# Expert weights kept in DRAM once as float32 and split into two parts when a unit is loaded

## The chip, the cores and the metric

The kernel runs on one core of one Trainium2 chip. The time is the device time of one execution in microseconds. The engines are called PE (TensorE), DVE (VectorE), ACT (ScalarE), POOL (GpSimd) and SP (SyncE, which here only issues DMAs).

## What is computed

Eight batches of attention whose 12 heads are mixed before and after the softmax, and behind it an expert layer on the 3584 tokens.

```python
scores = scale * np.matmul(q, k.transpose(0, 1, 3, 2))         # 8 x 12 x 448 x 448
scores = np.einsum('bhij,hg->bgij', scores, w_pre)
attn = softmax(scores)
attn = np.einsum('bhij,hg->bgij', attn, w_post)
x = np.matmul(attn, v)                                          # -> 3584 x 768
a, b = x @ w1, x @ w2                                           # 768 -> 1024
out = ((a * b) @ w3) @ w_out                                    # 1024 -> 1024 -> 768
```

## The kernel before

**Attention** goes in steps n; tile m of two blocks of 10 rows takes the two steps 2m and 2m+1. An even step fetches raw scores (`fetch`, L201), takes the largest value (`largest`, L226, DVE) and the exponentials (`exp`, L234, ACT); an odd step scales (`scale`, DVE and POOL), then multiplies with the second mixing matrix (`post`, L259, PE) and the next tile with the first (`mix`, L219, PE), copies the results (`put`, L273, ACT), and makes raw scores of the next batch (`qk`, L173, with two ACT copies, L178 and L179). `av` (L300) multiplies with v.

**The expert layer** is written as a generator whose steps are single PE matmuls. Each step n of the attention takes a number of them (`advance`), half before the exponentials are written and half behind, so expert matmuls fill PE between the attention's. The order in which instructions are written is the order on each engine; there is no planner. After the last attention step the rest runs alone, six matmuls at a time (the tail).

Matmuls take float32 numbers in two parts: `hi`, the number rounded by a copy to the type fp32r, and `lo`, the rest, by a subtract. Each product is three matmuls, hi x hi, hi x lo and lo x hi.

**Weights.** w3 and w_out are folded into one matrix at the start (`folding`, L359); w1 and w2 come as int64 words that are converted on the chip (`converting`, `to_f32`). Batches 0 and 1 go through the experts one at a time (`expert_atoms`, L521 and L552); batches 2 to 7 in three pairs (`pair_experts`), by a scheme with seven products m = 1 to 7 per block of two by two in place of eight (`layer`, L701). It needs sums of weight blocks; these are made once, while batch 1 passes (`seen`, `sums`).

A *unit* is the piece of weights of one matmul group or of half of one, 128 x 384 or 128 x 512 numbers in two parts. `wp` holds unit tiles (`wu`). `next_unit` hands out the next one and asks for a further load, which SP issues in the next step (`do_later`). At most `w_ahead` (3; for the pairs 4, in the tail 7) units are loaded or asked for ahead. A group's result stands in one of the two PSUM banks 6 and 7 in turn; `gather` (L655, DVE; its first product L657, ACT) adds it to an accumulator and frees the bank. It is written up to three matmuls after the next group has begun.

In DRAM everything lies in both parts: `w_d` (w1, w2), `w34_d` (the folded matrix), `s_d` (the sums). The parts are made where the numbers are made: by `two_parts` (ACT and POOL) for converted units, by an ACT copy and a DVE subtract for the folded matrix, by `split` (L482, L483: ACT and POOL) for the sums, eleven sets of four.

Of the kernel before, what the change touches and what calls it, by code (L numbers as in the profile page):

```python
# [49 lines left out]
class Kernel:  # L50
# [58 lines left out]
    def to_f32(self, s, m, name):  # L109
# [9 lines left out]
        x = self.cx.tile([128, CW], F32, tag="x", name=f"cx{name}")[:, :n]  # L119
# [227 lines left out]
    def folding(self):  # L347
        nc = self.nc
        for f in range(KF):
            for half in range(2):  # L350
# [10 lines left out]
                z = self.fp.tile([128, 3, 2, 128], F32R, tag="z", name=f"fz{half}_{f}")  # L361
                q = p.rearrange("p (d c) -> p d c", c=128)
                dst = self.w34_d[half * 3:(half + 1) * 3, :, f].rearrange("d p t c -> p d (t c)")

                def low(z=z, q=q, dst=dst):
                    nc.vector.tensor_tensor(z[:, :, 1], q, z[:, :, 0].bitcast(F32), op=ALU.subtract)
                    self.later.append(lambda: nc.sync.dma_start(dst, z.rearrange("p d t c -> p d (t c)").bitcast(F32)))

                self.ends.append((i, lambda z=z, q=q: nc.scalar.copy(z[:, :, 0], q)))
                self.soon.append((i, low))  # L370
# [17 lines left out]
    def load_unit(self):  # L388
        i = self.n_loaded
        t = self.wp.tile([128, KF // 2 * 256], F32R, tag="w", name=f"wu{i}")  # L390
        t, view, src = (self.unit_of_one if i < self.n_one else self.unit_of_pair)(t, *self.unit_list[i])
        self.nc.sync.dma_start(t.bitcast(F32), src)
        self.loaded.append(view)
        self.n_loaded += 1
        self.n_asked -= 1

    def unit_of_one(self, t, w, f, q):
        h = (K1 if w < 2 else KF) // 2
        t = t[:, :h * 256].rearrange("p (k t c) -> p k t c", k=h, t=2)
        return t, t, (self.w_d[w] if w < 2 else self.w34_d)[f][:, q * h:(q + 1) * h]  # L400

    def unit_of_pair(self, t, w, f, m):
        h, c = (K1 // 2, KF // 2) if w < 2 else (KF // 2, K1 // 2)
        t, src = t[:, :h * 256], self.w_d[w] if w < 2 else self.w34_d
        if m in (1, 2, 4):
            t = t.rearrange("p (k t c) -> p k t c", k=h, t=2)
            return t, t, src[f + c * (m == 4)][:, h * (m > 1):h * (1 + (m > 1))]
        return t, t.rearrange("p (t k c) -> p k t c", k=h, t=2), self.s_d[w][m][f]
# [8 lines left out]
    def unit_part(self, x, w, f, q):  # L417
        h = K1 // 2
        t = self.wp.tile([128, KF // 2 * 256], F32R, tag="w", name=f"wu{self.n_loaded}")
        t = t[:, :h * 256].rearrange("p (k t c) -> p k t c", k=h, t=2)  # L420
        self.loaded.append(t)
        self.n_loaded += 1
        self.two_parts(x, t[:, :, 0], t[:, :, 1])
        self.later.append(lambda: self.nc.sync.dma_start(self.w_d[w][f][:, q * h:(q + 1) * h], t.bitcast(F32)))

    def ask_units(self):
        while self.w_made <= self.n_loaded + self.n_asked < len(self.unit_list) and \
                len(self.loaded) + self.n_asked < self.w_ahead:
# [3 lines left out]
    def next_unit(self):  # L432

        t = self.loaded.pop(0)
# [33 lines left out]
    def sums(self, w, f, k):  # L468
# [8 lines left out]
        def split(m, i):  # L477
            s = self.cs.tile([128, CW, 2], I32, tag="s", name=f"s{w}_{f}_{m}", bufs=3)
            s = s.rearrange("p n b -> p (n b)").bitcast(F32)
            dst, x = self.s_d[w][m][f].rearrange("p (t n) -> p t n", t=2), y[:, i]  # L480
            hi, lo = s[:, :n], s[:, n:2 * n] if w < 2 else x
            nc.scalar.copy(hi.bitcast(F32R), x)  # L482
            nc.gpsimd.tensor_tensor(lo.bitcast(F32R), x, hi, op=ALU.subtract)  # L483
            if w < 2:
                self.later.append(lambda: nc.sync.dma_start(self.s_d[w][m][f], s))
            else:
                self.later.append(lambda: nc.sync.dma_start(dst[:, 0], hi))
                self.later.append(lambda: nc.sync.dma_start(dst[:, 1], lo))

        def first():  # L490
            sum(y[:, 0:2], y[:, 0:2], y[:, 2:4], ALU.subtract)

        def second():
            sum(y[:, 1:3], y[:, 1:3], y[:, 0::3], ALU.add)

        def third():
            sum(y[:, 3], y[:, 3], y[:, 0], ALU.subtract)


        splits = ((2, 7, 0), (3, 5, 2), (4, 3, 1), (5, 6, 3)) if w < 2 else ((3, 5, 2), (3, 3, 1), (4, 6, 3), (5, 7, 0))  # L500
        for delay, x in ((1, first), (2, second), (3 if w < 2 else 2, third)):
            self.at(delay, x)
        for delay, m, i in splits:
            self.at(delay, lambda m=m, i=i: split(m, i))
# [235 lines left out]
    def run(self):  # L740
# [9 lines left out]
        self.w_d = [dp.tile([KF, 128, k, 2, 128], F32, name=f"w{i}_d") for i, k in enumerate((K1, K1, KF))]  # L750
        self.x_d = [dp.tile([2, 128, K1 // 2, S], F32, name=f"x{b}_d") for b in range(B)]
        self.s_d = [{m: dp.tile([c, 128, k * 256], F32, name=f"s{i}_{m}_d") for m in (3, 5, 6, 7)}
                    for i, (c, k) in enumerate(((KF // 2, K1 // 2), (KF // 2, K1 // 2), (K1 // 2, KF // 2)))]
        self.w34_d = dp.tile([K1, 128, KF, 2, 128], F32, name="w34_d")
# [127 lines left out]
        self.loaded, self.n_loaded, self.n_asked, self.w_ahead = [], 0, 0, 3  # L882
# [5 lines left out]
        for n in range(N + 6):  # L888
# [4 lines left out]
            if n == SWITCH:  # L893
# [7 lines left out]
                self.wp = self.pool("wp", 5, side="right")  # L901
# [7 lines left out]
            if n == PAIR:  # L909
# [5 lines left out]
                self.pairs, self.w_ahead = True, 4  # L915
# [72 lines left out]
        self.wp, self.w_ahead = self.pool("wt", 8), 7  # L988
# [62 lines left out]
```

## Time and profile before

| | |
|---|---|
| three runs | 1453.31, 1459.1, 1459.4 us; median 1459.1 |
| profiled execution | 1456.61 us, span 1454.8 us, granted PE clock 0.985 |
| busy: PE, DVE, ACT, POOL | 1390.1, 739.0, 833.1, 620.7 us |
| DMA | 416.86 MB, mean 287 GB/s; HBM read 279.77 MB, written 134.09 MB |
| weight units loaded | 200 of 384 KB, 87 of 512 KB |

The span runs from the first to the last instruction of the profiled execution; the execution's time has 1.8 us more around it. Busy time is a union over the engine's instructions. In a list of waits each row names the engine and line that stood idle, what ended its wait, the sum in us, how often, and the longest. In a row of groups the number before the comma is busy time and the one after it the mean duration in ns. PE's busy time counts modelled ends of pipelined matmuls: one expert matmul stands with about 370 ns, but they start one every 0.2 us.

### The profile page before, as it was taken

The numbers are of one execution on the slowest core, as the hardware profiler recorded it, in microseconds if no ns is written. First come the engines' busy times: TensorE is split into PE (matmuls) and PEld (weight loads), VectorE is DVE, ScalarE is ACT, GpSimd is POOL, SyncE is SP. The second block draws the span as 40 slices with busy tenths as digits, with TensorE's granted clock in tenths as the row PEclk, the third lists the DMA queues.
The fourth block names the chain that finished last, engine by engine and source line by source line (L and its number), as shares of the span: only waits on it lengthen the run. The fifth ranks groups of instructions, "written<-read, shape, count | busy, mean of one in ns | idle before, by whom it ended". The sixth has DMA issues, their size and how long they took to land.

```text
span 1454.8 us, 45722 instructions
## 1 busy us (share of the span) xinstructions
PE 1390.1 (96%) x18684; PEld 1059.4 (73%) x18684; DVE 739.0 (51%) x1497; ACT 833.1 (57%) x1952; POOL 620.7 (43%) x754
## 2 busy tenths in 40 slices
PE   5789998999999989999999999999999999999998
PEld 2357785776677667776777777777776777899988
DVE  4867565767644544432344445334444447334563
ACT  3876665777756656665555656656655546422231
POOL 1333232444324434632244445444335446446683
PEclk7989998999999999999999999999999999999999
DMA  8998789999999999999989988799879766698875
GB/s 256 365 319 274 237 267 287 311 336 307 316 288 353 348 343 319 368 338 314 311 266 291 319 278 280 234 312 350 288 230 285 236 179 214 206 332 263 240 229 173
DMA packets 203760, 416.86 MB, mean 287 GB/s; under 512 B 20528, under 2 KB 120112, under 8 KB 203472
## 3 DMA queue, kind: packets, MB, share of 16 engines
q1 hardware_dynamic: 203552, 413.94, 87.2%
q8 instruction: 149, 2.44, 0.7%
q14 instruction: 59, 0.48, 0.1%
HBM read 279.77 MB, written 134.09 MB: 284 GB/s over the span
## 4 chain that ended last, share of the span: by engine, by line
PE 78%; DMA 13%; DVE 5%; ACT 3%; issue 1%; SPq 0%; POOL 0%; DVEq 0%; ACTq 0%; POOLq 0%
PE e L701 20%; PE psa L300 10%; PE pso L259 10%; PE psm L219 8%; PE psq L173 7%; PE psf L359 5%; PE eg L521 4%; PE e2o L701 4%; PE e1o L701 4%; PE e3o L701 4%; DMA s_d<-s 3%; PE eo L552 3%; DMA cs<-wo 3%; DMA r<-raw_d 2%; DMA wu<-w_d 2%; ACT e L234 1%
## 5 line engine op out<-in xcount | busy, mean ns | idle before, releaser
L246 POOL TENSOR_SCALAR w<-wpo,ri 128x60 f32<-128x60 f32 x360 | 180.7, 518 | 489.0 <-DVE ri L244 465.8
L226 DVE TENSOR_REDUCE mn<-psm 128x1 f32<-128x448 f32 x360 | 207.8, 619 | 317.0 <-PE psm L219 316.6
L701 PE MATMUL e<-eh,wu 128*128 128x448 f32 x1008 | 297.3, 372 | 6.3 <-DVE c L655 3.2
L273 ACT COPY mt<-pso 128x480 f32<-128x480 f32 x352 | 197.8, 621 | 177.3 <-PE pso L259 177.1
L234 ACT ACTIVATE e<-psm,mn 128x448 f32<-128x448 f32 x360 | 226.6, 642 | 9.6 <-DVE mn L226 9.6
L219 PE MATMUL psm<-r,wsc 60*64 60x448 f32 (+1 forms) x1440 | 197.9, 557 | 32.1 <-ACT e L234 19.9
L701 PEld LDWEIGHTS e<-eh,wu 128*128 128x128 f32 x1008 | 188.0, 188 | 52.5 <-issue 27.4
L259 PEld LDWEIGHTS pso<-w,e 60*64 60x64 f32 x10080 | 174.5, 134 | 50.0 <-issue 44.0
L259 PE MATMUL pso<-w,e 60*64 60x60 f32 x10080 | 198.6, 224 | 0.1
L701 PE MATMUL e<-el,wu 128*128 128x448 f32 x504 | 187.1, 371 | 0.0
L173 PE MATMUL psq<-kq 64*64 64x448 f32 x1176 | 159.5, 546 | 0.6 <-ACT st L178 0.6
L300 PE MATMUL psa<-mt,v 128*64 128x150 f32 (+1 forms) x2304 | 156.9, 293 | 1.9 <-ACT st L178 1.9
L300 PEld LDWEIGHTS psa<-mt,v 128*64 128x64 f32 x2304 | 143.6, 137 | 17.9 <-issue 6.3
L655 DVE TENSOR_TENSOR c<-c,e 128x448 f32<-128x448 f32 x168 | 101.8, 618 | 87.6 <-PE e L701 82.8
L178 ACT COPY st<-psq 128x448 f32<-128x448 f32 x162 | 86.4, 533 | 68.8 <-ACT mt L273 32.8
L521 PE MATMUL eg<-xh,wu 128*128 128x448 f32 x384 | 118.8, 380 | 4.8 <-DMA wu<-w_d 4.8
L640 POOL TENSOR_TENSOR el<-x,eh 128x448 fp32r<-128x448 f32 x90 | 104.2, 1176 | 34.8 <-ACT eh L639 34.8
L701 PEld LDWEIGHTS e<-el,wu 128*128 128x128 f32 x504 | 94.9, 188 | 22.4 <-issue 14.1
L243 DVE TENSOR_SCALAR sa<-sm 128x2 f32<-128x2 f32 x180 | 35.9, 200 | 129.6 <-ACT e L234 129.0
L173 PEld LDWEIGHTS psq<-kq 64*64 64x64 f32 x1176 | 62.2, 136 | 53.8 <-issue 29.8
L521 PEld LDWEIGHTS eg<-xh,wu 128*128 128x128 f32 x384 | 71.8, 190 | 38.1 <-issue 25.3
L179 ACT COPY st<-psq 128x448 f32<-128x448 f32 x162 | 87.7, 541 | 0.0
(99 smaller groups left out, 2011.5 us busy)
## 6 DMA issues: line engine op xcount, KB each, us to landing
r<-raw_d SPq DMA_DIRECT2D x344, 210.0 KB, 4.9
raw_d<-st SPq DMA_DIRECT2D x138, 448.0 KB, 5.4
wu<-w_d SPq DMA_DIRECT2D x104, 384.0 KB, 6.4
wu<-s_d SPq DMA_DIRECT2D x96, 384.0 KB, 4.8
wu<-w_d SPq DMA_DIRECT2D x51, 512.0 KB, 5.6
kq<-kq SPq DMA_DIRECT2D x42, 448.0 KB, 6.2
wu<-s_d SPq DMA_DIRECT2D x36, 512.0 KB, 4.9
x<-x_d SPq DMA_DIRECT2D x72, 224.0 KB, 6.3
```

Of the source, the lines that this page charges most:

```text
L173: nc.tensor.matmul(ps[s][z * PP:(z + 1) * PP], t[rows, q:q + PP], t[rows, k:k + S], start=True, stop=True)
L219: nc.tensor.matmul(ps[s][c * PP:(c + 1) * PP, :S], self.wsc[k], r[k, c], start=True, stop=True)
L226: self.nc.vector.tensor_reduce(mn[:, s:s + 1], self.psm[m][s][:, :S], axis=AX.X, op=ALU.min)
L234: nc.scalar.activation(e, p[:, :S], AF.Exp, bias=mn[:, s:s + 1], scale=-1.0, accum_out=sm[:, s:s + 1])
L246: nc.gpsimd.tensor_scalar_mul(w2[:, s], self.wpo, ri[:, s:s + 1])
L259: nc.tensor.matmul(self.pso[c][z * PP:(z + 1) * PP, at:at + HK], e[k, j * PP:(j + 1) * PP], w2s[k, s], start=True, stop=True)
L273: self.nc.scalar.copy(dst.rearrange("p j g (s i) -> p j s g i", s=2), src)
L300: nc.tensor.matmul(self.psa[rows, g % 3, :W], v[:, j, rows], mt[:, j, 2 * g + s, :W], start=(j == 0), stop=(j == NJ - 1))
L521: nc.tensor.matmul(p, u[:, k % (K1 // 2), x], xs[y][:, k], start=(k == 0 and t == 0), stop=(k == K1 - 1 and t == 2))
L640: nc.gpsimd.tensor_tensor(lo, x, hi.bitcast(F32), op=ALU.subtract)
L655: nc.vector.tensor_tensor(a[out], a[to[0]], p, op=ALU.add)
L701: nc.tensor.matmul(p, w[:, k, x], ops[m, k][y], start=(k == 0 and t == 0), stop=(k == nk - 1 and t == 2))
```

## The change

The weights, the folded matrix and the sums lie in DRAM once, as float32, in half the bytes. `load_unit` loads a unit into a raw tile (`wr`, pool `wr`). `split_unit` makes the two parts into the unit tile: an ACT copy (L415 of the changed kernel) and a subtract (L417), on POOL for the units of batches 0 and 1 and on DVE for those of the pairs. `next_unit` calls it until three units are split (one to hand out, `w_ready` = 2 ready; in the tail 3), and up to `w_ahead` = 3 (in the tail 5) raw ones are loaded or asked for besides. `wp` has 4 tiles in place of 5 and `wr` 4 (tail: 5 and 6 in place of 8). The sums and the folded matrix are stored as they are and no longer split when made; the first 32 units are still converted into both parts at once, and their float32 tile `cx` (three buffers, before two) is what is stored.

```diff
-        self.nc.sync.dma_start(t.bitcast(F32), src)
-        self.loaded.append(view)
+        x = self.wr.tile([128, KF // 2 * 128], F32, tag="r", name=f"wr{i}")[:, :h * 128]
+        self.nc.sync.dma_start(x, src)
+        self.raws.append((i, h, x))
...
+    def unit_tile(self, i, h):
+        t = self.wp.tile([128, KF // 2 * 256], F32R, tag="w", name=f"wu{i}")[:, :h * 256]
+        self.loaded.append(t.rearrange("p (k t c) -> p k t c", k=h, t=2))
+        return self.loaded[-1]
+
+    def split_unit(self):
+        i, h, x = self.raws.pop(0)
+        t, y = self.unit_tile(i, h), x.rearrange("p (k c) -> p k c", k=h)
+        self.nc.scalar.copy(t[:, :, 0], y)
+        low = self.nc.gpsimd if i < self.n_one else self.nc.vector
+        low.tensor_tensor(t[:, :, 1], y, t[:, :, 0].bitcast(F32), op=ALU.subtract)
...
-                len(self.loaded) + self.n_asked < self.w_ahead:
+                len(self.raws) + self.n_asked < self.w_ahead:
...
     def next_unit(self):
 
+        t = None
+        while self.raws and len(self.loaded) < 1 + self.w_ready:
+            self.split_unit()
         t = self.loaded.pop(0)
         self.ask_units()
         return t
...
-        def split(m, i):
-            s = self.cs.tile([128, CW, 2], I32, tag="s", name=f"s{w}_{f}_{m}", bufs=3)
...
-            nc.scalar.copy(hi.bitcast(F32R), x)
-            nc.gpsimd.tensor_tensor(lo.bitcast(F32R), x, hi, op=ALU.subtract)
...
+        def store(m, i):
+            self.later.append(lambda: nc.sync.dma_start(self.s_d[w][m][f], y[:, i]))
...
-                def low(z=z, q=q, dst=dst):
-                    nc.vector.tensor_tensor(z[:, :, 1], q, z[:, :, 0].bitcast(F32), op=ALU.subtract)
...
+                def leave(z=z, q=q, dst=dst):
+                    nc.scalar.copy(z, q)
+                    self.later.append(lambda: nc.sync.dma_start(dst, z))
...
-                self.wp = self.pool("wp", 5, side="right")
+                self.wp = self.pool("wp", 4, side="right")
+                self.wr = self.pool("wr", 4, side="right")
```

The order of PE's instructions stays as it is. What moves stands in the queues of ACT and DVE. First ACT in one period of the pairs (`mt` are the copies of `post`, `st` those of `qk`, `e` the exponentials, `eh` the hi parts of the next product's operands), before the change:

```order
L273 COPY mt_1_10434<-pso_142 128x4x2x12x5
L178 COPY st_4_1_10986<-psq_4_1_0_10980 128x448
L179 COPY st_4_1_10986<-psq_4_1_1_10981 128x448
L234 ACTIVATE e_0_11006,sm_11005<-psm_0_10972,mn_10993 128x448
L234 ACTIVATE e_1_11008,sm_11005<-psm_1_10973,mn_10993 128x448
L639 CAST eh_5_0_11032<-x_12_0_10109 128x448
```

The same place on ACT after the change:

```order
L273 COPY mt_1_10461<-pso_141 128x4x2x12x5
L178 COPY st_4_1_11040<-psq_4_1_0_11034 128x448
L179 COPY st_4_1_11040<-psq_4_1_1_11035 128x448
L415 CAST wu_11051<-wr_10875 128x3x128
L234 ACTIVATE e_0_11063,sm_11062<-psm_0_11026,mn_11047 128x448
L234 ACTIVATE e_1_11065,sm_11062<-psm_1_11027,mn_11047 128x448
L415 CAST wu_11070<-wr_10984 128x3x128
L641 CAST eh_5_0_11092<-x_12_0_10121 128x448
```

One cast of a unit stands between the copies of the scores and the exponentials, another behind the exponentials; which of them a period has depends on where the groups end in it.

DVE in the same period (`mn` the largest values, `c` the adds that free a bank, `sa` and `ri` the scaling), before the change:

```order
L226 TENSOR_REDUCE mn_10993<-psm_0_10972 128x1
L226 TENSOR_REDUCE mn_10993<-psm_1_10973 128x1
L655 TENSOR_TENSOR c_1_1_12_10582<-c_1_1_12_10582,e_6_1_1_10923 128x448
L655 TENSOR_TENSOR c_0_0_21_11017<-c_0_0_12_10366,e_7_0_0_10997 128x448
L243 TENSOR_SCALAR sa_11025<-sm_11005 128x2
L244 RECIPROCAL ri_11026<-sa_11025 128x2
```

The same place on DVE after the change:

```order
L226 TENSOR_REDUCE mn_11047<-psm_0_11026 128x1
L226 TENSOR_REDUCE mn_11047<-psm_1_11027 128x1
L417 TENSOR_TENSOR wu_11051<-wr_10875,wu_11051 128x3x128
L657 TENSOR_TENSOR c_1_1_12_10615<-c_1_1_12_10615,e_6_1_1_10977 128x448
L417 TENSOR_TENSOR wu_11070<-wr_10984,wu_11070 128x3x128
L657 TENSOR_TENSOR c_0_0_21_11077<-c_0_0_12_10390,e_7_0_0_11054 128x448
L243 TENSOR_SCALAR sa_11085<-sm_11062 128x2
L244 RECIPROCAL ri_11086<-sa_11085 128x2
```

Ahead of each add out of a PSUM bank (`c`) now stands the subtract of a unit that is used two groups later, and that subtract reads what the cast on ACT has written.

The third place is the tail, DVE again, one product of four groups (`t` are operands of the next product), before the change:

```order
L655 TENSOR_TENSOR c_0_0_12_19164<-c_0_0_12_19164,e_3_0_0_19492 128x448
L620 TENSOR_TENSOR t_0_19211<-x_21_0_18961,t_0_19211 128x448
L620 TENSOR_TENSOR t_1_19227<-x_21_1_18962,t_1_19227 128x448
L655 TENSOR_TENSOR c_0_1_12_19184<-c_0_1_12_19184,e_3_0_1_19514 128x448
L620 TENSOR_TENSOR t_2_19244<-x_21_2_18963,t_2_19244 128x448
L655 TENSOR_TENSOR c_1_0_12_19199<-c_1_0_12_19199,e_3_1_0_19538 128x448
L655 TENSOR_TENSOR c_1_1_12_19215<-c_1_1_12_19215,e_3_1_1_19558 128x448
```

The same product on DVE after the change:

```order
L657 TENSOR_TENSOR c_0_0_12_19656<-c_0_0_12_19656,e_3_0_0_20041 128x448
L622 TENSOR_TENSOR t_0_19712<-x_21_0_19426,t_0_19712 128x448
L417 TENSOR_TENSOR wu_20090<-wr_19989,wu_20090 128x3x128
L622 TENSOR_TENSOR t_1_19728<-x_21_1_19427,t_1_19728 128x448
L657 TENSOR_TENSOR c_0_1_12_19679<-c_0_1_12_19679,e_3_0_1_20066 128x448
L622 TENSOR_TENSOR t_2_19748<-x_21_2_19428,t_2_19748 128x448
L417 TENSOR_TENSOR wu_20113<-wr_20015,wu_20113 128x3x128
L657 TENSOR_TENSOR c_1_0_12_19697<-c_1_0_12_19697,e_3_1_0_20093 128x448
L417 TENSOR_TENSOR wu_20133<-wr_20030,wu_20133 128x3x128
L657 TENSOR_TENSOR c_1_1_12_19716<-c_1_1_12_19716,e_3_1_1_20116 128x448
```

Each of the groups has one subtract more, with two inputs in SBUF, as the operands' subtracts have.

64 lines of the change are left out of this document (26 added, 38 removed).

## Prediction

> **What bounds the kernel now.** I read the busy shares first, then the stages, then who kept TensorE waiting, and last one period of the steady loop. The first view is the page's list of busy time.
>
> ```profile
> PE 1390.1 (96%) x18684; PEld 1059.4 (73%) x18684; DVE 739.0 (51%) x1497; ACT 833.1 (57%) x1952; POOL 620.7 (43%) x754
> ```
>
> TensorE is busy for 1390.1 of 1454.8 us. No change of the other engines can give back more than its 65 us of idle time; any of them can add to it. The stages say where the idle time lies (columns: stretch, its length, busy us of each engine, granted clock, DMA share, GB/s).
>
> ```profile
> 0.00:100.00 100.00, 68.37 (x789) 33.51 (x791) 69.21 (x138) 64.11 (x149) 30.87 (x43) 0.86 0.96 324
> 235.00:260.00 25.00, 19.17 (x256) 12.40 (x251) 15.40 (x33) 14.79 (x35) 9.75 (x13) 0.80 0.93 309
> 450.00:695.00 245.00, 234.46 (x3533) 171.87 (x3531) 103.05 (x224) 152.24 (x364) 100.91 (x123) 0.99 1.00 340
> 695.00:1010.00 315.00, 314.19 (x4554) 241.08 (x4555) 135.21 (x296) 189.31 (x444) 135.98 (x176) 1.00 0.90 291
> 1010.00:1095.00 85.00, 83.97 (x1239) 64.09 (x1238) 34.77 (x79) 51.13 (x121) 31.15 (x43) 1.00 0.85 271
> 1095.00:1293.00 198.00, 194.18 (x2656) 155.68 (x2655) 93.55 (x188) 98.52 (x232) 101.63 (x121) 0.99 0.74 229
> 1293.00:1399.00 106.00, 104.48 (x508) 95.02 (x507) 60.47 (x85) 24.79 (x49) 68.20 (x56) 1.00 0.85 273
> ```
>
> Half of the idle time is in the first 100 us, which the change hardly touches. From 450 to 695 us the DMA engines are full (1.00) and 10.5 us are lost. From 695 us on, where the pairs of batches run, TensorE loses 0.8, 1.0, 3.8 and 1.5 us: almost nothing is left to win, and everything the change adds there must hide.
>
> **What the halved bytes can give.** The waits of TensorE in 450 to 700 us, then the two of 1095 to 1293 us, then ACT's own wait for the stores of the split sums, and the wait at 240 us:
>
> ```profile
> PE eg L521 <- DMA wu<-w_d: 4.8, 3, 2.7
> PE psm L219 <- ACT e L234: 3.3, 5, 1.1
> PE psm L219 <- DMA r<-raw_d: 2.2, 1, 2.2
> ...
> PE e L701 <- DMA wu<-w_d: 2.4, 1, 2.4
> PE e L701 <- DVE c L655: 1.4, 3, 0.8
> ...
> ACT s L482 <- DMA s_d<-s: 13.8, 7, 2.8
> ...
> ACT cm L106 <- DMA cs<-w: 6.8, 1, 6.8
> ...
> wu<-w_d SPq DMA_DIRECT2D x104, 384.0 KB, 6.4
> wu<-s_d SPq DMA_DIRECT2D x96, 384.0 KB, 4.8
> wu<-w_d SPq DMA_DIRECT2D x51, 512.0 KB, 5.6
> wu<-s_d SPq DMA_DIRECT2D x36, 512.0 KB, 4.9
> ```
>
> 287 loads move 200 x 384 + 87 x 512 KB = 121 MB; half of that, 61 MB of the page's 417, goes, and half of the stores of weights, fold and sums (about 18 MB). In 450 to 695 us it is some 18 MB (32 units and as many stored sums at 192 KB, 12 of each at 256) of 83 (340 GB/s), so the full DMA engines get about a fifth of slack. There the waits for weights (4.8) and for score rows (2.2) should mostly vanish, and the splits of the sums go altogether, with ACT's wait behind their stores, which holds up the exponentials that TensorE waits for (3.3). With the slower clock after a stall (0.99 of 245 us is 2.4 us) I take **-9**, between 0 (the backlog stays) and -12. At 1114 us one wait for weights of 2.4 us and the clock behind it (0.99 of 198 us): **-2**, between 0 and -4. At 240 us ACT stands for 6.8 us behind a load of the int64 weights, which is as large as before; two stores ahead of it are halved, 0.4 MB at 340 GB/s: **-1.5** (0 to -3). The first 100 us: one or two halved stores of the folded matrix and no DVE half of its split: **-0.5**. On SP, the store of a converted unit no longer stands behind POOL (the first row below); nothing in that stage waits for SP, so nothing. Sum of the gains: **-13**, between 0 and -20.
>
> **What it adds.** Each of the 287 loads now brings an ACT copy (`hi`) and a subtract (`lo`): on POOL for the 56 units of the first two batches, on DVE for the 231 units of the pairs. These operations exist today on the same shapes (mean ns is the second number after the bar):
>
> ```profile
> SPq L424 <- POOL wu L126: 33.4, 23, 4.8
> ...
> L125 ACT CAST wu<-cx 128x384 fp32r<-128x384 f32 x32 | 16.9, 527 | 0.0
> L482 ACT CAST s<-y 128x512 fp32r<-128x512 f32 x12 | 7.2, 630 | 3.1 <-DMA s_d<-s 3.1
> L483 POOL TENSOR_TENSOR y<-y,s 128x512 fp32r<-128x512 f32 x12 | 15.3, 1284 | 14.0 <-ACT s L482 13.9
> L462 DVE TENSOR_TENSOR y<-wu 128x384 f32<-128x384 f32 x32 | 17.1, 553 | 2.4 <-DMA wu<-w_d 2.4
> L462 DVE TENSOR_TENSOR y<-wu 128x512 f32<-128x512 f32 x12 | 8.1, 676 | 0.2 <-DMA s_d<-s 0.2
> ```
>
> ACT: 200 x 0.527 + 87 x 0.630 = 160 us, less 44 such copies for the sums (24 us). DVE: 168 x 0.553 + 63 x 0.676 = 135 us, less 16 of 0.553 in the fold (9 us). POOL: 56 more and 44 fewer, 12 x 1.284 = 15 us. As busy time it all fits: between 695 and 1293 us about 152 units come, 82 us on ACT beside 339 of 598 and 86 us on DVE beside 264. The question is where they stand, since each engine works in the order in which its instructions are written.
>
> *The first two batches.* ACT does as many casts as before in 450 to 695 us, and each group takes both of its units, so a bank has 18 matmuls of time. The twelve units of the folded matrix between 400 and 480 us are new ACT work ahead of exponentials: **+1** (0 to +4).
>
> *The pairs, 695 to 1293 us.* Here is one period (start and length in us; the mixing matmuls, the start of the run of 18 expert matmuls, the next mixing, then ACT, then DVE, and at the end two rows of a period without score copies):
>
> ```profile
> 740.58 0.98 PE L219 MATMUL psm<-r,wsc 60*64 60x448 f32 x7
> ...
> 742.24 0.67 PE L701 MATMUL e<-eh,wu 128*128 128x448 f32 x2
> ...
> 746.95 0.98 PE L219 MATMUL psm<-r,wsc 60*64 60x448 f32 x7
> ...
> 742.77 0.54 ACT L179 COPY st<-psq 128x448 f32<-128x448 f32 x1
> 743.19 0.65 ACT L234 ACTIVATE e<-psm,mn 128x448 f32<-128x448 f32 x1
> ...
> 744.33 0.22 ACT L234 ACTIVATION_READ_ACCUMULATOR e<-psm,mn 128x1 f32 x1
> ...
> 742.75 0.62 DVE L655 TENSOR_TENSOR c<-c,e 128x448 f32<-128x448 f32 x1
> 744.57 0.62 DVE L655 TENSOR_TENSOR c<-c,e 128x448 f32<-128x448 f32 x1 [1.20 <-PE e L701]
> 745.11 0.16 DVE L243 TENSOR_SCALAR sa<-sm 128x2 f32<-128x2 f32 x1
> ...
> 1201.85 0.67 PE L701 MATMUL e<-eh,wu 128*128 128x448 f32 x2
> 1201.95 1.16 DVE L226 TENSOR_REDUCE mn<-psm 128x1 f32<-128x448 f32 x2 [1.56 <-PE psm L219]
> ```
>
> The run starts at 742.24; a matmul comes every 0.205 us (104.48 us for 508 in the last of the stages). One group ends after its first matmul, the next lasts 9, and the one after that (from matmul 10, at 744.28) needs the PSUM bank of the first. Today DVE adds the first group out of its bank at 742.75, done by 743.37: 0.9 us to spare. In the new order (shown under the change) the subtract of a unit stands ahead of that add, and it needs ACT's cast, which stands behind the two score copies: cast 743.19 to 743.72, subtract to 744.32, add to 744.85 (DVE starts its next operation 0.54 after an add, 744.57 to 745.11). TensorE waits until then, 2.6 us into the run in place of matmul 10's 2.04: **0.56 us lost** in this period. Where the cast falls behind the two exponentials (1.23 us more) the release comes at 3.85 us. I counted the places in the new order by the matmul at which the second next group starts. With score copies (to 1095 us): matmul 9 in 2 places (0.76 each), 10 in 4 (0.56), 11 in 6 (0.35), 12 in 3 (0.15), and behind the exponentials 16 in 1 (0.56) and 17 in 4 (0.35): 8.3 us. In 11 places, five of them not among these, another DVE operation (a second add, or a subtract for the next operands) stands in between, 0.54 each time: 6.2 us more. Without score copies the cast runs earlier, but the subtract waits for the two reductions (1201.95 + 1.16 is 1.26 us into the run that starts at 1201.85), and the release is at 2.35 or 3.7 us: 12 places, 6.1 us. Together **+20**; the lower end is 4 (the 0.5 us of each cast hidden after all, as it would be with ACT ahead of the score copies), the upper 30 (a POOL operation in the way of every third subtract). I take 20 because each duration in it is that of a row of this loop. The exponentials themselves move by one cast, and the mixing of the next tile starts 2.4 us after they end (744.55 to 746.95), so they cost nothing.
>
> *The tail, from 1293 us.* TensorE runs expert groups alone, one per 1.85 us, and DVE and POOL are both busy:
>
> ```profile
> L620 DVE TENSOR_TENSOR x<-x,x x18: 605/619/1579, 699.2 to 1348.5; 128x448 f32<-128x448 f32 x18
> L620 DVE TENSOR_TENSOR x<-t,x 128x448 f32<-128x448 f32 x6 | 6.4, 1069 | 0.0
> L640 POOL TENSOR_TENSOR el<-x,eh x90: 1127/1147/1638, 679.5 to 1372.2; 128x448 fp32r<-128x448 f32 x90
> ```
>
> A DVE subtract of two SBUF tiles takes 0.62 us alone and up to 1.58, and POOL's subtract 1.15 alone and up to 1.64, when they meet. The Trainium skill, page "SBUF — State Buffer", section "SBUF: two separate sides", says that VectorE instructions with two SBUF inputs and GpSimd's hold one port pair exclusively, each for the whole instruction. The lengthened rows agree with waiting, not with sharing at half speed. New in 1293 to 1399 us are 54 subtracts, 54 x 0.553 = 30 us on DVE's 60.5 of 106: it fits if none meets POOL (0), and if each meets it as those in the tail do (1.07 less 0.62, 0.45 each, 24 us more) the sum is 115, 9 us too many. POOL is busy for two thirds of the stretch, so I take **+5** for the whole tail, with ends 0 and +12.
>
> **Sum.** -13 + 1 + 20 + 5 = +13. The profiled execution took 1456.6 us (span 1454.8), 2.5 under the median of the three runs, 1459.1. So 1456.6 + 13 = **1470 us**. About 0.5%, 7 us, is what a measurement of this kernel can tell from no change.
>
> **Rivals.**
> 1. *Faster: the adds are not late.* If cast and subtract of a unit end about 0.6 us earlier after a run's start than I count, most of the 38 places have no shortfall and the 20 becomes 4; then -13 + 1 + 4 + 5 = -3, and with the full gain of -20 it is 1447. For it: ACT has 40% of idle time; against it: the ACT rows above, where the cast has no earlier place. From about 0.4 us less per place it decides. 1449, chance 0.18.
> 2. *No change:* the loss in the loop is half of what I count and the gains are as taken, 1459, within 0.5%: 0.30.
> 3. *The raw unit lands late, and ACT stands before it.* The cast comes three units after its load was asked for, where the load had four before; ACT then holds up exponentials, which have 2.4 us to spare. In the loop the loads are issued a period (6.4 us) or more ahead and land in about 5, with fewer bytes; 20 late ones of 1 us beyond the spare time would give 1490. Chance 0.10.
> 4. *The port decides in the tail:* 1293 to 1399 us becomes bound by DVE and POOL taking turns, +14 in place of +5 with the last stretch to 1455: 1479. By the page named above this is how it must go wherever the two overlap; the rows above bear out the waiting, not how often it will happen. Chance 0.10.
> My forecast has 0.32. Slower by over 0.5%, above 1466: forecast, 3 and 4, 0.52; within: 0.30; faster, under 1452: 0.18. The range 1447 to 1488 leaves out about 0.2: the far end of 1 and most of 3. The likeliest case's own range is 1464 to 1478.
>
> **What will show it.** The loss in the loop: a wait of `e` matmuls for the DVE add of some 20 us in total (1.4 us stands in the list of 1095 to 1293 us), in pieces of 0.2 to 1.5 us, and busy TensorE below 0.98 in 695 to 1293 us. The gains: the waits for `wu` gone from TensorE's list, a DMA share near 0.8 in 450 to 695 us, and no `s` copies. The tail: the DVE add waiting less for TensorE and `el` on POOL well over 1.25 us. Wrong if TensorE's waits for DVE stay under 8 us, or if ACT's list shows waits of many us for the raw tiles.

## The result and the profile after

The changed kernel takes 1508.6 us (median of four runs, 1503.1 to 1511.5) against 1457.0 for the kernel before in the same job: a ratio of 1.0358 (1.0332 to 1.0383). The forecast was 1470 with a range up to 1488. The profiled execution took 1509.55 us, its span is 1507.7.

The page's list of busy time, and the stretches of the changed kernel that answer to the last five of those shown before (the columns are as there: stretch, length, busy us of PE, PEld, DVE, ACT, POOL, granted clock, DMA share, GB/s):

```profile
PE 1403.9 (93%) x18684; PEld 1053.6 (70%) x18684; DVE 899.5 (60%) x1712; ACT 944.7 (63%) x2195; POOL 658.9 (44%) x766
...
455.00:682.00 227.00, 225.68 (x3527) 168.18 (x3526) 114.24 (x226) 155.42 (x371) 109.24 (x131) 1.00 0.87 280
682.00:1025.00 343.00, 324.20 (x4553) 240.80 (x4554) 183.47 (x373) 223.66 (x523) 139.65 (x175) 0.99 0.71 222
1025.00:1115.00 90.00, 86.55 (x1248) 64.76 (x1247) 47.03 (x102) 61.07 (x146) 31.82 (x43) 1.00 0.66 201
1115.00:1320.00 205.00, 192.54 (x2641) 151.04 (x2640) 131.09 (x243) 120.33 (x282) 107.99 (x119) 1.00 0.54 159
1320.00:1446.00 126.00, 111.22 (x515) 97.42 (x514) 103.66 (x142) 52.81 (x108) 75.31 (x59) 0.97 0.41 128
```

The first stretch is 18 us shorter than before (227 against 245) and has almost no idle time left. Every later one is longer: 343 against 315, 90 against 85, 205 against 198, 126 against 106. No engine but PE is near full in any of them except DVE in the last, 103.7 of 126.

For all kernels below, the table compares the moment at which the exponentials of a tile start with the same moment in the kernel before (us, later is positive; each number is a difference of two start times of the ACT rows `e<-psm`). Tile 60 is at 444 us in the kernel before, tile 100 at 716, where the pairs run already, tile 179, the last, at 1260. The last two columns are differences of those before them: the loop of the pairs, and the tail behind the last tile. Each row is one profiled execution. The changed kernel, e5_tail_psum and e7_tail_sbuf are the same program up to tile 179, and their loops stand at 38.0, 34.7 and 38.0, so a difference of 3 us between two rows need not mean anything.

| kernel | tile 60 | tile 100 | tile 179 | end | loop | tail |
|---|---|---|---|---|---|---|
| changed kernel | 4.3 | -12.9 | 25.1 | 52.9 | 38.0 | 27.8 |
| e1_add_first | 3.5 | -15.0 | -17.8 | 1.2 | -2.8 | 19.0 |
| e2_no_sub | 3.1 | -15.2 | -20.1 | -20.7 | -4.9 | -0.6 |
| e6_lag | 0.7 | -17.7 | -8.5 | 4.0 | 9.2 | 12.5 |
| e5_tail_psum | 1.3 | -15.2 | 19.5 | 20.8 | 34.7 | 1.3 |
| e7_tail_sbuf | 3.4 | -14.0 | 24.0 | 34.5 | 38.0 | 10.5 |
| e8_raw_in_psum | 2.8 | -16.1 | -19.1 | -9.2 | -3.0 | 9.9 |
| e9_first_lag | 1.9 | -16.2 | -19.0 | -5.8 | -2.8 | 13.2 |
| e10_four_banks | -1.4 | -18.7 | -21.6 | -5.0 | -2.9 | 16.6 |
| e11_lag_psum | 2.5 | -16.1 | -18.9 | -17.2 | -2.8 | 1.7 |
| e12_lag_psum_banks | 2.6 | -15.9 | -18.6 | -17.7 | -2.7 | 0.9 |
| e13_extra_bytes | 4.6 | -12.6 | -15.3 | 3.7 | -2.7 | 19.0 |
| e14_sum_splits | 7.6 | -5.9 | -8.6 | 11.1 | -2.7 | 19.7 |

So the change had gained 13 us by tile 100, then lost 38 in the loop and 28 in the tail. In the tail PE waits for DVE's adds as well; here is its longest wait in the kernel before (1260 to 1399 us) and in the changed one (1285 to 1447 us):

```profile
PE e L701 <- DVE c L655: 1.5, 1, 1.5
```

```profile
PE e L703 <- DVE c L657: 11.6, 8, 2.8
```

In the loop, the waits of PE and of DVE in the changed kernel from 703 to 1285 us, and one line's own row there (min/median/max ns):

```profile
PE e L703 <- DVE c L657: 21.1, 22, 2.9
PE e L703 <- ACT e L234: 3.0, 6, 0.8
PE e1o L703 <- DVE sa L243: 1.9, 1, 1.9
PE e1o L703 <- DVE c1o L657: 1.8, 3, 0.8
...
DVE wu L417 <- ACT wu L415: 96.7, 87, 2.8
...
L417 DVE TENSOR_TENSOR wu<-wr,wu x139: 545/559/1701, 704.5 to 1280.6; 128x384 fp32r<-128x384 f32 x105, 128x512 fp32r<-128x512 f32 x34
```

PE now waits for DVE's adds (`c` L657), as forecast, and DVE's subtract stood 97 us waiting for ACT's cast. A wait counts only PE's modelled idle time; by the starts of successive expert matmuls, an interval was more than 0.15 us above the usual one, and ended by one of DVE's operations or by the exponentials, in 41 places, 36.8 us in all. The largest of them, in order of time on PE, DVE and POOL:

```profile
902.33 0.37 PE L703 MATMUL e<-eh,wu 128*128 128x448 f32 x1
905.62 0.44 PE L703 MATMUL e<-eh,wu 128*128 128x448 f32 x1 [2.93 <-DVE c L657]
...
901.85 1.62 DVE L417 TENSOR_TENSOR wu<-wr,wu 128x512 fp32r<-128x512 f32 x1 [1.16 <-ACT wu L415]
903.40 1.55 DVE L622 TENSOR_TENSOR c<-c,c 128x448 f32<-128x448 f32 x1
904.87 0.61 DVE L657 TENSOR_TENSOR c<-c,e 128x448 f32<-128x448 f32 x1
...
901.78 4.16 POOL L642 TENSOR_TENSOR el1o<-c,eh1o 128x448 fp32r<-128x448 f32 x3
```

PE stops at 902.33 for want of a bank. The add that frees it stands behind a subtract that waited 1.16 us for its cast and then took 1.62 us, and behind one more DVE operation of 1.55, both while POOL was at three subtracts in a row.

Theories for the experiments: (1) place: the adds are late because they stand behind subtracts that wait for casts; (2) load and port: DVE has too much to do, since its operations lengthen when they meet POOL's; (3) the raw units land late.

### The profile page after: what moved, and what is told of

Its sections match the earlier page's. It is cut to its first block, busy times and chain, and to the rows that moved or that the text cites. A ratio compares the mean times of both kernels' runs of the same rounds, so it can differ in the third digit from the quotient of the medians.

```text
span 1507.7 us, 46503 instructions
## 1 busy us (share of the span) xinstructions
PE 1403.9 (93%) x18684; PEld 1053.6 (70%) x18684; DVE 899.5 (60%) x1712; ACT 944.7 (63%) x2195; POOL 658.9 (44%) x766
## 5 line engine op out<-in xcount | busy, mean ns | idle before, releaser
L703 PE MATMUL e<-eh,wu 128*128 128x448 f32 x1008 | 309.7, 378 | 42.3 <-DVE c L657 32.7
L417 DVE TENSOR_TENSOR wu<-wr,wu 128x384 fp32r<-128x384 f32 (+1 forms) x231 | 186.7, 809 | 135.2 <-ACT wu L415 134.3
L219 PE MATMUL psm<-r,wsc 60*64 60x448 f32 (+1 forms) x1440 | 193.1, 555 | 27.1 <-ACT e L234 16.1
L415 ACT CAST wu<-wr 128x384 fp32r<-128x384 f32 (+1 forms) x287 | 157.2, 553 | 48.6 <-issue 17.6
L417 POOL TENSOR_TENSOR wu<-wr,wu 128x384 fp32r<-128x384 f32 (+1 forms) x56 | 72.3, 1291 | 125.0 <-ACT wu L415 119.3
L178 ACT COPY st<-psq 128x448 f32<-128x448 f32 x162 | 86.5, 534 | 62.7 <-ACT mt L273 38.3
L642 POOL TENSOR_TENSOR el<-x,eh 128x448 fp32r<-128x448 f32 x90 | 108.2, 1215 | 39.4 <-ACT eh L641 31.6
L657 DVE TENSOR_TENSOR c<-c,e 128x448 f32<-128x448 f32 x168 | 101.0, 613 | 10.8 <-PE e L703 9.2
```

Source lines behind the costliest of these rows:

```text
L219: nc.tensor.matmul(ps[s][c * PP:(c + 1) * PP, :S], self.wsc[k], r[k, c], start=True, stop=True)
L415: self.nc.scalar.copy(t[:, :, 0], y)
L417: low.tensor_tensor(t[:, :, 1], y, t[:, :, 0].bitcast(F32), op=ALU.subtract)
L703: nc.tensor.matmul(p, w[:, k, x], ops[m, k][y], start=(k == 0 and t == 0), stop=(k == nk - 1 and t == 2))
```

## The experiments

Each ratio is to the kernel before in the same job, with its 95% interval. The edits are against the changed kernel; in the profile rows each kernel has its own line numbers.

**The add ahead of the subtract.**

```diff
     def next_unit(self):
+        if self.pairs:
+            self.do_ends()
         while self.raws and len(self.loaded) < 1 + self.w_ready:
             self.split_unit()
```

`do_ends` writes what is still to be written of finished groups: DVE's add, or ACT's copy for a first product.

> From the pairs on, the pending add of a finished group is written ahead of the cast and the subtract of the next unit. Theory 1 (place in DVE's row): the adds are late because they stand behind a subtract that waits for ACT's cast; with the add in front, the loss between the tiles 100 and 179 (now 38 us) falls to under 12 us, the tail (now 28 us) by some 10 us at most, and the time is 1470 to 1485 us. Theory 2 (load and port): DVE has the same work and meets POOL as often; the loss stays within 8 us of what it is and the time is 1500 to 1510 us. Theory 3 (raw units late): no change, 1505 to 1510 us.

1458.3 us, ratio 1.0037 (1.0020 to 1.0053). The loop's loss is gone altogether (-2.8 us where the changed kernel has +38), the tail's falls from 28 to 19. PE's wait for the adds from 700 to 1242 us, then PE's longest waits, DVE's subtract and POOL in the tail, 1242 to 1398 us (mean ns is the second number after the bar):

```profile
PE e L705 <- DVE c L659: 1.0, 3, 0.4
...
PE e L705 <- ACT eh L643: 5.4, 5, 1.2
PE e L705 <- DVE c L659: 4.9, 10, 1.5
...
L417 DVE TENSOR_TENSOR wu<-wr,wu 128x384 fp32r<-128x384 f32 (+1 forms) x67 | 59.7, 893 | 13.6 <-ACT wu L415 13.4
...
L686 POOL TENSOR_TENSOR c<-c,c 128x448 f32<-128x448 f32 x15 | 20.6, 1371 | 10.8 <-DVE c L659 10.8
```

It is better than theory 1 had said. DVE does the same work in the loop as in the changed kernel, so there it never lacked capacity: the order was the whole loss. In the tail PE now waits as long for the high parts of the next product's operands (`eh`) as for the adds; ACT makes them from what DVE has subtracted before.

**No subtracts.**

```diff
-        low = self.nc.gpsimd if i < self.n_one else self.nc.vector
-        low.tensor_tensor(t[:, :, 1], y, t[:, :, 0].bitcast(F32), op=ALU.subtract)
+        if i < self.n_one:
+            self.nc.gpsimd.tensor_tensor(t[:, :, 1], y, t[:, :, 0].bitcast(F32), op=ALU.subtract)
...
-                    nc.tensor.matmul(p, w[:, k, x], ops[m, k][y],
+                    nc.tensor.matmul(p, w[:, k, 0], ops[m, k][y],
```

> Leaves out the subtracts of the pairs' 231 units: the third product of each weight uses the high part again, so TensorE, ACT and the transfers do what they did, and the low part of the weights is missing from the result. Theories 1 and 2 both put the whole loss of 66 us on these subtracts: 1442 to 1452 us, with under 5 us of loss between the tiles 100 and 179 and under 5 us in the tail. Theory 3 (raw units late, ACT standing before them): the loss stays, over 1490 us.

1436.9 us, ratio 0.989 (0.987 to 0.991), a little below what was expected. Loop -4.9, tail -0.6: the casts on ACT and the new loads cost nothing by themselves, and the whole loss of 66 us (38 and 28) goes with the subtracts and what they hold up. This speaks against theory 3, whose loss would have stayed; ACT's list of waits from 703 to 1285 us in the changed kernel has no wait for a raw tile either.

**The subtract one unit behind its cast.**

```diff
-        low.tensor_tensor(t[:, :, 1], y, t[:, :, 0].bitcast(F32), op=ALU.subtract)
+        todo, self.lag = self.lag, [lambda: low.tensor_tensor(t[:, :, 1], y, t[:, :, 0].bitcast(F32), op=ALU.subtract)]
+        if not self.pairs:
+            todo, self.lag = todo + self.lag, []
+        for f in todo:
+            f()
...
         t = self.loaded.pop(0)
+        if not self.raws and self.lag:
+            self.lag.pop(0)()
```

> In the pairs, the subtract of a unit is written one unit later than its cast, ahead of the next unit's cast, so that DVE never stands waiting for a cast; subtracts, adds and their number are as they were, and an add still stands behind a subtract of some 0.6 to 0.9 us. Theory 1: the waiting is the cost; the DVE wait for ACT in the subtract's line (134 us in all, 118 places) falls under 20 us, the loss between the tiles 100 and 179 from 38 to under 15 us, and the time to 1475 to 1488 us. Theory 2: the subtracts themselves and their meeting with POOL are the cost: the loop keeps over 25 us of its loss and the tail all of it: 1497 to 1510 us.

1464.0 us, ratio 1.0077 (1.0047 to 1.0108). PE's wait and the subtract's row in the loop (698 to 1251 us), then the subtract in the tail (1251 to 1401 us):

```profile
PE e L709 <- DVE c L663: 10.4, 9, 1.8
...
L417 DVE TENSOR_TENSOR wu<-wr,wu 128x384 fp32r<-128x384 f32 (+1 forms) x139 | 106.1, 764 | 0.9 <-ACT wu L415 0.6
...
L417 DVE TENSOR_TENSOR wu<-wr,wu 128x384 fp32r<-128x384 f32 (+1 forms) x68 | 64.4, 950 | 5.8 <-ACT wu L415 5.6
```

The wait for the cast is gone from the loop (0.6 us in place of 97), and 29 of its 38 us with it. The 9 that stay are adds behind subtracts that do not wait but are long: nine waits, 10.4 us. In the tail the subtract is as long as ever, and 12.5 of 28 us stay.

**The tail: the subtract's second input in PSUM, and then in SBUF.**

```diff
         self.nc.scalar.copy(t[:, :, 0], y)
         low = self.nc.gpsimd if i < self.n_one else self.nc.vector
-        low.tensor_tensor(t[:, :, 1], y, t[:, :, 0].bitcast(F32), op=ALU.subtract)
+        hi = t[:, :, 0].bitcast(F32)
+        if self.zero is not None:
+            hi = self.zero[:, :h * 128].rearrange("p (k c) -> p k c", k=h)
+        low.tensor_tensor(t[:, :, 1], y, hi, op=ALU.subtract)
...
         self.w_ahead, self.w_ready = 5, 3
+        self.zero = self.ps.tile([128, 512], F32, tag="b2", name="zero")
+        nc.vector.memset(self.zero, 0.0)
```

In e7_tail_sbuf the tile comes from a pool of SBUF instead.

> In the tail alone, the subtract's second input is a bank of PSUM full of zeros in place of the high part in SBUF (so the low parts hold the whole value there). DVE does as many subtracts of the same size, with one SBUF input, and none of them waits for ACT's cast. Theory 2 (in the tail DVE and POOL hold one port in turn): the subtract falls from 896 ns to under 700, POOL's 1420 ns row to under 1250, and the tail's loss of 28 us falls to under 12: 1490 to 1497 us. Theory 1 (waiting for the cast): the wait of 10 us for ACT goes, and no duration changes; the tail's loss falls by 5 us or less if DVE's load sets it, by 10 if the wait does: 1498 to 1505 us. The loop before the tail stays as it is.

> As e5_tail_psum, but the bank of zeros is a tile of SBUF: in the tail the subtracts still wait for no cast (and the low parts hold the whole value), while both of their inputs are in SBUF again. The two kernels differ in the home of one input. If the port that DVE and POOL share sets the tail, the subtract takes 850 to 950 ns as in the changed kernel against 561 in e5_tail_psum, and the tail's loss is 10 to 20 us against 1: 1487 to 1500 us. If the waits for the cast set it, the tail's loss stays under 5 us: 1478 to 1484 us.

1481.3 us, ratio 1.0200 (1.0175 to 1.0225), with PSUM; 1489.4 us, ratio 1.0247 (1.0216 to 1.0277), with SBUF. The subtract and POOL's multiply in the tail of the one (1279 to 1420 us) and of the other (1281 to 1434 us):

```profile
L420 DVE TENSOR_TENSOR wu<-wr,zero 128x384 fp32r<-128x384 f32 (+1 forms) x63 | 35.2, 561 | 5.5 <-DMA wr<-w_d 3.5 <-PE e L706 1.5 <-issue 0.2
...
L687 POOL TENSOR_TENSOR c<-c,c 128x448 f32<-128x448 f32 x15 | 18.1, 1205 | 5.9 <-DVE c L660 5.9
```

```profile
L420 DVE TENSOR_TENSOR wu<-wr,zero 128x384 fp32r<-128x384 f32 (+1 forms) x63 | 59.6, 948 | 3.3 <-DMA wr<-w_d 2.2 <-PE e L706 0.6 <-issue 0.4
...
L687 POOL TENSOR_TENSOR c<-c,c 128x448 f32<-128x448 f32 x15 | 21.3, 1420 | 5.7 <-DVE c L660 5.7
```

Neither waits for a cast. With one input in PSUM the subtract takes 561 ns and the tail loses 1.3 us; with both in SBUF it takes 948 ns and the tail loses 10.5. So meeting POOL costs this tail 9 us by itself (7 by the two ratios). Both theories had a part: the other 17 of the changed kernel's 28 go when the waits for the cast go.

**Repairs of the tail.** e8 is e1_add_first with

```diff
+        if self.tail:
+            p = self.bank(i % 2 + 2, f"wb{i}")[:, :h * 128]
+            self.nc.scalar.copy(p, x)
+            y = p.rearrange("p (k c) -> p k c", k=h)
         self.nc.scalar.copy(t[:, :, 0], y)
```

e9 is e1_add_first and e6_lag together, and e10 is e1_add_first with four banks for the tail's groups:

```diff
         self.n_groups += 1
+        if self.tail:
+            return (2, 6, 3, 7)[self.n_groups % 4]
         return 6 + self.n_groups % 2
```

> The whole result again: the add first from the pairs on (as e1_add_first), and in the tail ACT also copies each raw unit into a bank of PSUM, from which ACT's cast and DVE's subtract read it. ACT gets 54 more copies, some 30 us on 68 busy of 156. Theory 2 (port in the tail): the subtract falls to 560 to 620 ns, the tail's loss from 19 us (e1_add_first) to under 5: 1437 to 1444 us, faster than the kernel before. If the waits for the cast set the tail: the subtract waits for two ACT operations in place of one, and the loss stays at 15 to 25 us: 1455 to 1465 us.

> The whole result: the add first (e1_add_first) and the subtract one unit behind its cast (e6_lag), so that neither engine's row holds a wait for the other. If what is left in the tail is waiting, both together take its loss under 8 us: 1440 to 1447 us. If it is the load of DVE and POOL on their port, the loss stays at 10 to 19 us: 1448 to 1458 us.

> The whole result: the add first (e1_add_first), and in the tail the expert groups go round four banks of PSUM in place of two, so that an add may be two groups later before TensorE waits. If the tail's loss is adds that come late one at a time, it falls from 19 us to under 6: 1438 to 1446 us. If DVE and POOL cannot do the tail's work in TensorE's time, the lateness adds up, and four banks put it off by two groups (some 4 us) only: 1450 to 1457 us.

1448.6 us (ratio 0.997, 0.995 to 0.999), 1452.9 (0.9996, 0.9979 to 1.0012) and 1454.0 (1.0001, 0.9985 to 1.0018). The subtract in the tails of e8 (1243 to 1390 us), e9 and e10 (both 1245 to 1394 us):

```profile
L421 DVE TENSOR_TENSOR wu<-wb,wu 128x384 fp32r<-128x384 f32 (+1 forms) x63 | 35.8, 567 | 24.6 <-ACT wu L419 24.6
```

```profile
L417 DVE TENSOR_TENSOR wu<-wr,wu 128x384 fp32r<-128x384 f32 (+1 forms) x67 | 55.5, 831 | 3.6 <-ACT wu L415 3.6
```

```profile
L417 DVE TENSOR_TENSOR wu<-wr,wu 128x384 fp32r<-128x384 f32 (+1 forms) x66 | 60.5, 918 | 13.7 <-ACT wu L415 13.5
```

e8 and e9 each take away one cause and keep the other; e10 keeps both. In e8 the subtract is short and waits 25 us for two ACT operations: the tail keeps 9.9, over the 5 that theory 2 had set and under the other theory's 15. In e9 the subtract waits little (3.6 us) and stays long: 13.2 stay, as the port's case said. In e10 the banks move the loss: at the start of the last products (`e3o`) it is 13.8 us ahead of the kernel before, at the end 5.0, and the time is that of its second case. PE's list there has no add any more; it waits for the low and high parts of the operands (1245 to 1394 us):

```profile
PE e L707 <- POOL el L646: 2.8, 4, 0.8
PE e L707 <- ACT eh L645: 1.7, 3, 0.9
```

So DVE's lateness reaches PE by a second way, the operands of the next product, which more banks do not help.

**Both causes taken away.** e11 has the add first in the loop, the raw unit through PSUM and the subtract one unit behind its cast in the tail; e12 has the add first in the tail and four banks there as well. Their edits are those above, with the lag in the tail alone and banks 0, 6, 1 and 7 in e12.

> The whole result: the add first in the loop of the pairs (as e1_add_first); in the tail the raw unit goes through PSUM (as e8_raw_in_psum), the subtract stands one unit behind its cast (as e6_lag), and the add keeps its old place. If the tail's loss is the sum of the two causes, waiting for the cast and DVE and POOL meeting on their port, both are gone here and the tail loses under 5 us, as in e5_tail_psum (1 us), against 10 in e8_raw_in_psum: 1438 to 1444 us. If ACT, which gets a copy and a cast a unit, becomes late for the operands' high parts, the tail keeps 6 to 12 us: 1445 to 1451 us.

> The whole result: e11_lag_psum with the add first in the tail too, and four banks for its groups. If late adds are what is left after e11_lag_psum, this brings the tail's loss under 3 us: 1436 to 1441 us. If the loss comes from the operands of the next phase (ACT's high parts, POOL's low parts), banks change nothing: within 2 us of e11_lag_psum.

1439.8 us (ratio 0.9901, 0.9872 to 0.9930) and 1439.7 (0.9904, 0.9871 to 0.9937): faster than both kernels, by 1.0% and by 4.6% (1439.8 against 1508.6, in different jobs). PE's wait for adds and the subtract in the tail of e11 (1241 to 1380 us), and the same stretch of e12 (columns as in the stretches above):

```profile
PE e L715 <- DVE c L669: 1.5, 2, 1.3
...
L421 DVE TENSOR_TENSOR wu<-wb,wu 128x384 fp32r<-128x384 f32 (+1 forms) x60 | 33.4, 559 | 9.2 <-ACT wu L419 9.1
```

```profile
1241.00:1380.00 139.00, 138.25 (x835) 124.60 (x834) 100.84 (x166) 95.18 (x202) 86.62 (x75) 1.00 0.54 166
```

The tail loses 1.7 and 0.9 us, and PE is busy for 138 of 139 us with DVE at 101 and ACT at 95. The four banks and the add first in the tail add nothing that can be told from chance once both causes are gone. The result of e12 fits both of its cases, so it does not tell them apart.

**Where the gain comes from.** e13 copies each of the 56 units of the first two batches once more, from DRAM to DRAM, on the same queue; e14 puts the split of each stored sum back as extra work. Both are built on e1_add_first.

```diff
         self.nc.sync.dma_start(x, src)
+        if i < self.n_one:
+            self.nc.sync.dma_start(self.scratch[i % 8][:, :h * 128], src)
```

```diff
+        def split(m, i):
+            s = self.cs.tile([128, CW, 2], I32, tag="s", name=f"s{w}_{f}_{m}", bufs=3)
+            s = s.rearrange("p n b -> p (n b)").bitcast(F32)
+            hi, lo = s[:, :n], s[:, n:2 * n] if w < 2 else s[:, :n]
+            nc.scalar.copy(hi.bitcast(F32R), y[:, i])
+            nc.gpsimd.tensor_tensor(lo.bitcast(F32R), y[:, i], hi, op=ALU.subtract)
+            dst = self.scratch[(f + i) % 8][:, :n]
+            self.later.append(lambda: nc.sync.dma_start(dst, lo))
...
+        for delay, m, i in ((2, 7, 0), (3, 5, 2), (4, 3, 1), (5, 6, 3)):
+            self.at(delay, lambda m=m, i=i: split(m, i))
```

> e1_add_first with each of the 56 units of the first two batches also copied once more, from its place in DRAM to a scratch place in DRAM on the same queue, so that the bytes of these loads are at least what they were in the kernel before; the result is whole and no engine has more to compute. If the gain between the tiles 60 and 100 (17 to 19 us in every kernel with raw units) comes from the halved loads, 8 to 18 us of it go and the time is 1464 to 1476 us; if it comes from the splits of the sums that are gone from ACT and POOL and from their smaller stores, it stays within 4 us: 1456 to 1462 us.

> e1_add_first with the old splitting of the 44 stored sums put back as extra work beside it: for each sum an ACT copy, a POOL subtract and a store of the result to a scratch place (so the bytes of these stores are what they were); the sums themselves are stored and used as in e1_add_first. If the gain between the tiles 60 and 100 came from the splits (ACT held behind stores, 13.8 us in the kernel before, and the exponentials behind ACT), 8 to 18 us of it go: 1464 to 1476 us, and TensorE waits for ACT's exponentials there again. If it needs the full DMA engines as well (341 GB/s before), the gain stays within 4 us here as it did with the loads copied twice: 1456 to 1463 us.

1460.1 us (ratio 1.0037, 1.0014 to 1.0059) and 1464.4 (1.0071, 1.0047 to 1.0094). Stretches of e1_add_first, e13 and e14, and ACT's wait behind the stores in e14:

```profile
450.00:680.00 230.00, 229.38 (x3575) 170.98 (x3563) 116.42 (x229) 158.64 (x377) 110.13 (x131) 1.00 0.87 278
```

```profile
450.00:680.00 230.00, 229.81 (x3604) 170.33 (x3603) 115.54 (x228) 156.41 (x373) 109.74 (x132) 1.00 0.97 320
```

```profile
450.00:695.00 245.00, 242.79 (x3713) 180.08 (x3711) 131.48 (x238) 182.18 (x432) 159.33 (x177) 1.00 0.94 310
...
ACT s L511 <- DMA sc_d<-s: 9.6, 8, 2.5
```

Between tiles 60 and 100 e1_add_first gains 18.5 us, e13 17.2, e14 13.5; the changed kernel and the other nine, which have the same work there, lie between 16.5 and 18.9. With the DMA engines at 0.97 again the gain stays, so it is not their slack by itself. What e13 does not put back is the length of the loads that PE needs: each is half as large there too. The splits take some 5 us of the gain (the two ratios differ by 5 us as well, but their intervals overlap), between the two cases; ACT waits behind their stores again (9.6 us against 13.8), but PE's wait for the exponentials comes back with 1.1 us only. Where most of the 18 us comes from is open.

## Why the prediction was wrong, point by point

That it gets slower, and by adds that come late, was forecast; two prices of the sum failed. A place in the loop was priced at 0.53 us and cost 0.90, and the tail was priced as busy time, with the wait for the cast put at nothing: 5 us forecast, 26 to 28 measured.

- **The gains, -13 + 1: nearly right in sum, not in their places.** Without the -2 that I had put at 1114 us, -10 was due by tile 100, and -12.9 came. Up to tile 30 (at 261 us in the kernel before) it was -2.2 where I had -2. From tile 60 to 100 it was -17.2 where I had -9 with an end at -12; from tile 30 to 60 it was +6.5 where I had +1 with an end at +4. The kernels here that differ only later lie between +3.0 and +7.7 in that last stretch, so some 4 us of it are not told from a rerun. That the slack of the DMA engines would carry the gain is not borne out (e13).
- **The pair loop, +20 with an upper end of 30: the failing size.** The mechanism is the forecast one: e1_add_first, which moves only what frees the banks, takes the loss away whole. The 38 us already hold the gain that I had put at 1114 us (the loops with the add first stand at -2.8), so the loss is nearer 41. The number of places was right too, 38 counted (the list gives 37, and its 11 x 0.54 is 5.9, not 6.2) and 41 found, 12 of them past the last score copies, as counted. What was wrong is the price of a place: 20/38 = 0.53 us counted, 36.8/41 = 0.90 found. In the 3.5 us before the 41 releases the subtracts and DVE's other operations with two SBUF inputs were 11.7 us longer in all than their usual shortest; without these the sum is 25 of 37, and the 5 us that it is still above 20 stay open. I had priced the subtract at its 553 and 676 ns of the kernel before. Its median from 703 to 1285 us is 559, but its mean 715, and single ones take up to 1701. I priced lengthening by POOL in the tail alone, and it also works here, at the places where it hurts: of the 128x384 subtracts of that loop, the 72 that overlap no POOL instruction in the timeline take at most 561 ns, the 33 that overlap one take 847 in the mean and up to 1487. DVE's adds, with one input in PSUM, stay between 605 and 620 ns either way.

```profile
L417 DVE TENSOR_TENSOR wu<-wr,wu 128x384 fp32r<-128x384 f32 (+1 forms) x139 | 99.3, 715 | 97.2 <-ACT wu L415 96.7
```

- **The tail, +5 with an upper end of 12: the step that failed outright.** From 1293 us on, where the forecast has it begin, it cost 26 us (126 us in place of 106 in the stretch with the groups, and 6 behind it). It was priced as a sum of busy time (30 us more on DVE's 60.5 of 106), and the wait for the cast was left out, though the order in the tail is the same as in the loop. The busy time itself did not run over: DVE has 103.7 of 126 us. But two groups of matmuls take 3.7 us, so an add that comes that late stops PE. By e7_tail_sbuf the meeting with POOL costs 10.5, near rival 4's +14, and the wait for the cast the other 17 of the 28. By e8_raw_in_psum waiting without the meeting costs 9.9, though with the add in front and two ACT operations to wait for. So the two cost more together than each by itself; that a subtract which waits for a cast and then for POOL holds the add twice is my reading, which no run shows apart. About 3 us of the 28 are of a third kind, which I had not priced in the tail. From 1347.5 and from 1443.1 us, behind waits of PE of 1.9 and 2.8 us, the granted clock is 0.5 for 3.4 us, and 16 matmuls start 0.37 us apart in place of 0.205.
- **Rival 1 (adds not late)** is out: PE's waits for the adds are 21.1 us in the loop. **Rival 2 (half the loss)** is out with it.
- **Rival 3 (raw units late)** is out: e2_no_sub has the same loads and casts and loses nothing.
- **Rival 4 (the port in the tail)** had one of the tail's two causes right, and its size about right.
- **What was to show it.** PE's waits for DVE's adds of some 20 us came as 21.1, with pieces of up to 2.9 us in place of 1.5. The share of DMA near 0.8 came as 0.87, PE waits for no `wu` from 455 to 682 us (its list there is empty), and no copy `s` is left in the stage of the sums. In the tail DVE's adds wait 9.2 us for PE in place of 38.0. `el` on POOL "well over 1.25 us" did not come: POOL's multiply is lengthened (1420 ns against 1223 before), the most frequent `el` hardly (1277 against 1241). In these meetings it was DVE that stood longer: 929 ns for the subtract.

```profile
L417 DVE TENSOR_TENSOR wu<-wr,wu 128x384 fp32r<-128x384 f32 (+1 forms) x68 | 63.0, 929 | 24.4 <-ACT wu L415 24.2
...
L684 POOL TENSOR_TENSOR c<-c,c 128x448 f32<-128x448 f32 x15 | 21.3, 1420 | 9.5 <-DVE c L657 8.4 <-ACT eh3o L641 1.0
```

(Both are rows of the changed kernel from 1285 to 1447 us; the 1223 is POOL's same row in the kernel before, 1260 to 1399 us.)

## What to carry to other kernels

When a change adds an instruction to an engine that also frees PSUM banks, write the instruction that frees the bank first, and put at least one unit between a producer on one engine and its consumer on another: here the same work in another order was worth 50 us, and the change showed as a gain (1%) only once the order was mended and, in the tail, the subtract read its input from PSUM. Count the places where a bank comes late and price each with the new operation as it runs beside its neighbours, not as it ran alone. And price every stage in which the new order stands, not only the one where it was first seen.

## What the runs showed of the hardware

In the tail a DVE subtract of two SBUF tiles takes 0.93 to 0.95 us in the mean beside a busy POOL, for what takes 0.56 alone; with one of its inputs in PSUM it stays at 0.56 in the same place, beside the same POOL operations (e5 against e7, e11 against the changed kernel). How they meet can be read in four rows of the changed kernel's timeline (start and length in us):

```profile
832.74 1.47 DVE L622 TENSOR_TENSOR x<-t,x 128x448 f32<-128x448 f32 x1
834.13 1.49 DVE L417 TENSOR_TENSOR wu<-wr,wu 128x384 fp32r<-128x384 f32 x1
...
832.57 1.16 POOL L642 TENSOR_TENSOR el<-x,eh 128x448 fp32r<-128x448 f32 x1 [2.05 <-ACT eh L641]
833.68 1.52 POOL L684 TENSOR_TENSOR c<-c,c 128x448 f32<-128x448 f32 x1
```

POOL's subtract ends at 833.73, and DVE's operation that began meanwhile ends 0.48 us later, at 834.21, most of its length alone (0.62). POOL's multiply, begun at 833.68, ends 0.99 us after that, at 835.20, and DVE's subtract, begun at 834.13, another 0.42 later, at 835.62. Each record is long by about the time in which the other engine had its turn, and no list of waits shows it as idle time.

The Trainium skill, page "SBUF — State Buffer", section "SBUF: two separate sides", says that a VectorE instruction with two SBUF inputs and a GpSimd instruction that reads SBUF hold the shared pair of ports one at a time, each to its end. These runs agree (what is left of each instruction above comes to its length alone less 0.1 to 0.2 us), and show that moving one input to PSUM takes the instruction out of it. The price of that way is one ACT copy a unit, which ACT could bear in the tail (95 us busy of 139 in e12), and two PSUM banks.
